# Long FFT convolution and phase mixing on Trainium2: the start of the kernel, with its trigonometric tables, written anew

## Chip, cores and metric

The kernel runs on one core of one Trainium2 chip. The metric is device microseconds of one execution; the median of three runs stands for a kernel. A time is compared with the kernel before, run on the same chip.

## What is computed

Eight sequences of 5696 tokens with 128 channels are convolved causally, channel by channel, with a filter `h` of the same length. The result goes through a phase mixing layer.

```python
def _attn_ref(x, h):                      # x (8, 5696, 128), h (5696, 128)
    L = 2 * S
    y = np.fft.irfft(np.fft.rfft(x, n=L, axis=1) * np.fft.rfft(h, n=L, axis=0)[None], n=L, axis=1)[:, :S, :]
    return y

def _moe_ref(x, w_theta, w_tok_r, w_tok_i, w_ch):
    theta = x @ w_theta
    zr, zi = x * np.cos(theta), x * np.sin(theta)
    y = np.einsum('ts,bsd->btd', w_tok_r, zr) + np.einsum('ts,bsd->btd', w_tok_i, zi)
    u = x + y
    return u + np.maximum(u @ w_ch, 0.0)
```

The output is that of the second function on the result of the first, in float32.

## The kernel before

**The convolution** is a Fourier transform of length 11392 = 178 x 64 in matrix multiplications. The inputs are cut into eight groups (two sequences, half the channels), and `h` is handled first as if it were a group. A group goes through four stages. *Stage a* (`stage_a`, L198) multiplies 89 rows by a table `f1_t` of 90 frequencies: 16 chunks of four matmuls (L207), each evicted from PSUM with 128x720 elements (L212 on VectorE or L214 on ScalarE). *Stage f2* (`f2`, L217) does the 64-point transform and the twiddle factors in one: for each of the 90 frequencies a weight of its own from `w_t2`, four matmuls of 64 rows a frequency (L225), eight frequencies a chunk, so 12 chunks, the last with two frequencies. After the last chunk the function issues 12 matmuls of 384 columns whose results nobody uses (L231, `WARM`), into the same PSUM tile as the last chunk; that chunk's eviction comes after them. For `h` the chunks are evicted, alternating between ScalarE (L262) and VectorE (L260), and written to HBM (L267, two transfers a chunk on SP's queue); for a group of `x`, *stage b* (`stage_b`) evicts them on ScalarE (L323), multiplies them on VectorE (L325, L330) by the spectrum of `h`, which SP's queue reads back (L316, two transfers a chunk, four chunks ahead), and fills `uv_t`. *Stages c and d* (L346 and following) transform back with tables `r_u`, `r_v`, `e_t` and the signs `sgn`. PSUM has four buffers for all of this.

**The tables.** All of them are sines and cosines of a turn, built on the chip. `turns_of` (L156) makes an index with an iota on GpSimd (L163), scales it there to a fraction of a turn (L165), and takes the nearest whole turn off on VectorE (L168, L169). `sine` is a ScalarE activation (L173); `cosine` takes the absolute value on VectorE (L176) and then an activation (L180). `w_table(k0)` (L190) does this for 15 frequencies of `w_t2`, 15 x 64 = 960 columns, and writes the negative of the sine with L195; six of them cover the 90 frequencies. The tiles `turn` and `whole` have two buffers each. A weight of `w_t2` is 128 rows (two copies of 64) by three blocks of 64 columns: sine, cosine, minus sine.

**The order.** The program writes: `f1_t`, three `w_table`, the copy of `h` into `h16` (L245, one instruction), the loads of x for groups 0 and 1 (`load_x`, L143, 16 transfers each on GpSimd's queue, which cast to 16 bits), stage a of `h` with the other three `w_table` woven in, the 12 chunks of f2 for `h` (`h_chunk`), then stage a of group 0 with `r_table`, `s_table` and the first loads of the spectrum woven in, and stage b of group 0 with three `e_table` woven in. The compiler's planner is free to put independent instructions of an engine in another order; the trace shows the order that it chose. From `setup.close()` (L403) on, the loop over the groups weaves stages c and a, then b and d. The program's later part has a stretch in which VectorE keeps its written order (`manual_schedule`, L949); the setup has none.

**The mixing** takes what is left: weights are streamed through a ring (L530), transposed on VectorE (L731), and multiplied in seven products in place of eight (L1116). It is not touched.

Of the kernel before, what the change touches and what calls it, by code (L numbers as in the profile page):

```python
# [10 lines left out]
F32 = mybir.dt.float32  # L11
BF16 = mybir.dt.bfloat16
F16 = mybir.dt.float16
add = mybir.AluOpType.add
# [8 lines left out]
def kernel(  # L23
# [10 lines left out]
    nc = tc.nc  # L34
# [48 lines left out]
    EN = N2 // 2 + 1  # L83
    WARM = 12
    XP = HD + 2
    assert N1 * N2 == NF and NB * N2 == S and NB % 2 == 1 and K1 <= P
    CHK = [(c0, min(CK, K1 - c0)) for c0 in range(0, K1, CK)]
    NCK = len(CHK)
# [14 lines left out]
    def pool(name, bufs, stack, **kw):  # L103
        return stack.enter_context(tc.tile_pool(name=name, bufs=bufs, **kw))
# [6 lines left out]
    fc = pool("fft_c", 1, conv, side="right")  # L111
    fs = pool("fft_s", 2, conv, side="right")
    s1 = pool("set_1", 1, setup, side="right")
    s2 = pool("set_2", 2, setup, side="right")

    uv_t = fc.tile([P, 2 * UVW + P], F16)
    u_t, v_t = uv_t[:, :UVW + P], uv_t[:, UVW:]
# [9 lines left out]
    def load_x(g, after=None):  # L127

        bp, dh = divmod(g, 2)
        if g >= B:  # L130
            return []
        if g not in x16s:
            x16s[g] = fx.tile([P, 2, N2, XP], F16, tag="x16", name="x16")
        x16 = x16s[g]

        def piece(i):
            e, n0 = i // 4, i % 4 * 16
            src = x[2 * bp + e]
            if after is not None:
                g_ = after["g"]  # L140
                nc.gpsimd.tensor_copy(x16[0:1, e, n0, 0:1], g_[0:1, 0, 16 * i:16 * i + 1])  # L141
            for p0, p1 in ((0, 80), (80, NB)):
                nc.gpsimd.dma_start(  # L143
                    x16[p0:p1, e, n0:n0 + 16, :HD],
                    bass.AP(tensor=src.tensor, offset=src.offset + (p0 * N2 + n0) * D + dh * HD,
                            ap=[[N2 * D, p1 - p0], [D, 16], [1, HD]]))
        return [lambda i=i: piece(i) for i in range(8)]

    lane = fc.tile([P, 2], F32)
    for p0 in (0, 64):  # L150
        nc.gpsimd.iota(lane[p0:p0 + 64, 0:1], pattern=[[0, 1]], base=0, channel_multiplier=1,
                       allow_small_or_imprecise_dtypes=True)
    nc.gpsimd.iota(lane[:, 1:2], pattern=[[0, 1]], base=0, channel_multiplier=1,
                   allow_small_or_imprecise_dtypes=True)

    def turns_of(pattern, base, lanes, m, per, quarter=None):  # L156

        n = 1
        for _, c in pattern:
            n *= c  # L160
        t = s2.tile([P, 11 * NB], F32, tag="turn", name="turn")[:m, :n]
        k = s2.tile([P, 11 * NB], F32, tag="whole", name="whole")[:m, :n]
        nc.gpsimd.iota(k, pattern=pattern, base=base, channel_multiplier=0,  # L163
                       allow_small_or_imprecise_dtypes=True)
        nc.gpsimd.tensor_scalar(t, k, lanes, 1.0 / per, op0=mult, op1=mult)  # L165
        if quarter is not None:
            quarter(t)
        nc.vector.tensor_scalar(k, t, MAGIC, None, op0=add)  # L168
        nc.vector.scalar_tensor_tensor(t, k, MAGIC, t, op0=ALU.subtract, op1=ALU.subtract)  # L169
        return t, k  # L170

    def sine(out_, r, sign):
        nc.scalar.activation(out_, r, AF.Sin, bias=zero_b[:r.shape[0]], scale=-sign * TWO_PI)  # L173

    def absolute(k, r):
        nc.vector.scalar_tensor_tensor(k, r, -1.0, r, op0=mult, op1=ALU.max)  # L176

    def cosine(out_, r, k):
        absolute(k, r)
        nc.scalar.activation(out_, k, AF.Sin, bias=half_pi[:r.shape[0]], scale=-TWO_PI)  # L180

    f1_t = fc.tile([P, 2 * K1], F16)
    t, k = turns_of([[1, K1]], 0, lane[:NB, 1:2], NB, N1)
    sine(f1_t[:NB, K1:], t, -1)
    cosine(f1_t[:NB, :K1], t, k)

    w_t2 = keep.tile([P, K1, 3 * N2], F16, tag="keep", name="w_t2")
    assert WB + BT + 3 * P * 2 <= K1 * 3 * N2

    def w_table(k0):  # L190
        t, k = turns_of([[1, 15], [N1, N2]], k0, lane[:, 0:1], P, NF)
        t3, k3 = (z.rearrange("p (k n) -> p k n", n=N2) for z in (t, k))
        sine(w_t2[:, k0:k0 + 15, :N2], t3, 1)
        cosine(w_t2[:, k0:k0 + 15, N2:2 * N2], t3, k3)
        nc.vector.tensor_scalar(w_t2[:, k0:k0 + 15, 2 * N2:], w_t2[:, k0:k0 + 15, :N2],  # L195
                                -1.0, None, op0=mult)

    def stage_a(lhs, both=False):  # L198

        st = {}  # L200

        def chunk(q):
            if q == 0:
                st["a"] = fa.tile([P, 2 * K1, HD], F16, tag="a", name="a_")
            ps = psum()
            for i in range(4):
                nc.tensor.matmul(ps[:, i // 2, (i % 2) * 2 * K1:(i % 2 + 1) * 2 * K1], lhs(q + i), f1_t[:NB],  # L207
                                 start=True, stop=True)
            a_out = st["a"][:, :, q:q + 4].rearrange("p k (a q) -> p k a q", a=2)
            a_in = ps[:, :, :4 * K1].rearrange("p a (q k) -> p k a q", q=2)  # L210
            if both and q % 8:
                nc.vector.tensor_copy(a_out, a_in)  # L212
            else:
                nc.scalar.activation(a_out, a_in, AF.Copy)  # L214
        return [lambda q=q: chunk(q) for q in range(0, HD, 4)], st
# [19 lines left out]
    def woven(*lists):  # L235

        lists = [l if isinstance(l, tuple) else (l, 0.0, 1.0) for l in lists]
        steps = [(w0 + (i + 0.5) / len(l) * (w1 - w0), n, f)
                 for n, (l, w0, w1) in enumerate(lists) for i, f in enumerate(l)]
        for _, _, f in sorted(steps, key=lambda s: s[:2]):  # L240
            f()

    for k0 in (0, 15, 30):
        w_table(k0)
    nc.vector.tensor_copy(h16[:NB], u_t[:NB, :N2 * D].rearrange("p (n h d) -> p h n d", h=2, d=HD))  # L245
    for f in load_x(0) + load_x(1):
        f()
    steps, a_h = stage_a(lambda q: h16[:NB].rearrange("p h n d -> p (h n) d")[:, :, q], True)
    woven(steps, [lambda k0=k0: w_table(k0) for k0 in range(45, K1, 15)])

    hst = [t[:, :6 * D * CK].rearrange("p (c h d k) -> p c h d k", c=6, h=2, k=CK) for t in (u_t, v_t)]
    nc.gpsimd.memset(hst[(NCK - 1) // 6][:, (NCK - 1) % 6], 0.0)
# [1 line left out]
    def h_chunk(c):  # L254
        c0, ck = CHK[c]
        ps = f2(a_h, c)
        h_ = hst[c // 6][:, c % 6]
        dst = h_[:, :, :, :ck]
        if c % 2:
            nc.vector.tensor_scalar(dst, ps, 16.0 / NF, None, op0=mult)  # L260
        else:
            nc.scalar.activation(dst, ps, AF.Copy, scale=16.0 / NF)  # L262
        for cc, j in ((0, 0), (NCK - 1, CHK[-1][1] - 1)):
            if c == cc:
                nc.vector.tensor_scalar(dst[:, :, :, j], dst[:, :, :, j], 0.5, None, op0=mult)
        for ri in range(2):
            nc.sync.dma_start(  # L267
                hf_hbm[:, c, :, ri, :].rearrange("h p n -> p h n"),
                h_[64 * ri:64 * ri + 64].rearrange("p h d k -> p h (d k)"))

    for c in range(NCK):
        h_chunk(c)
    nc.gpsimd.memset(uv_t[:, 2 * UVW:], 0.0)

    r_u = fc.tile([P, P], F16)
    r_v = fc.tile([P, P], F16)
    e_t = fc.tile([P, EN, 2, NB], F16)
    sgn = fc.tile([P, N2], F32)

    def r_table(n_, r_):  # L280
        def quarter(t):
            for q0 in range(2):
                for q1 in range(2):
                    a_ = t[64 * q0:64 * q0 + 64, 64 * q1:64 * q1 + 64]
                    nc.vector.tensor_scalar(a_, a_, 0.25 * (1 + n_ + q0 - q1), None, op0=add)

        t, k = turns_of([[0, 2], [1, N2]], 0, lane[:, 0:1], P, N2, quarter)
        sine(k, t, 1)
        nc.vector.tensor_scalar(r_[:, :N2 + EN], k[:, :N2 + EN], 0.125, None, op0=mult)
        nc.vector.tensor_scalar(r_[:, N2 + EN:], k[:, N2 + EN:], -0.125, None, op0=mult)  # L290

    def e_table(n0):
        t, k = turns_of([[1, 11], [N2, NB]], n0, lane[:K1, 1:2], K1, NF)
        t3, k3 = (z.rearrange("p (n m) -> p n m", m=NB) for z in (t, k))
        sine(e_t[:K1, n0:n0 + 11, 1, :], t3, -1)
        cosine(e_t[:K1, n0:n0 + 11, 0, :], t3, k3)

    def s_table():
        t, k = turns_of([[0, 1]], 1, lane[:, 1:2], P, 2)
        absolute(k, t)  # L300
        nc.vector.tensor_scalar(k, k, -4.0, 1.0, op0=mult, op1=add)
        nc.vector.memset(sgn, 1.0)
        nc.vector.tensor_scalar(sgn[:, EN:], sgn[:, EN:], k, None, op0=mult)

    LEAD = 4

# [82 lines left out]
    zz_n, ZB = [0], 3  # L389
    groups = [(bp, dh) for bp in range(B // 2) for dh in range(2)]  # L390

    def front(g):
        if g >= len(groups):
            return [], [], []
        bp, dh = groups[g]
        x16 = x16s[g].rearrange("p b n d -> p (b n) d")
        steps, a_st = stage_a(lambda q: x16[:NB, :, q])
        return (steps, *stage_b(a_st, dh))

    a0, load0, b0 = front(0)  # L400
    woven(a0, [lambda: r_table(0, r_u), lambda: r_table(1, r_v), s_table] + load0)
    woven(b0, [lambda n0=n0: e_table(n0) for n0 in range(0, EN, 11)])
    setup.close()  # L403
    fg = pool("fft_g", 1, conv, side="right")

# [773 lines left out]
```

## Time and profile before

| | us |
|---|---|
| runs: lowest, median, highest | 2082.85, 2087.07, 2088.17 |
| the profiled execution, device time | 2088.55 |
| its span, first to last instruction | 2086.7 |
| granted TensorE clock over the span | 0.984 |
| TensorE (PE) busy | 1955.1 |
| VectorE (DVE), ScalarE (ACT), GpSimd (POOL) busy | 1587.1, 646.6, 972.5 |

PE is busy for 94% of the span. A profile names the matmul's records PE and the weight loads PEld. A line of the timeline has the start, the duration, the engine, the source line and the operation with its tiles and sizes, how many there were, and in brackets the idle time of the engine before it with what ended it. A run of like instructions is merged into one line. Lines of the view by stretches have, for each engine in turn, busy time and number of instructions, then the granted clock, the share of the DMA engines and the rate.

### The profile page before, as it was taken

How to read it: one execution, taken by the hardware profiler on the slowest of the kernel's cores; microseconds unless marked ns; L12 is line 12 of the kernel's file. 1: busy time of each engine (PE TensorE's matmuls, PEld its weight loads, DVE VectorE, ACT ScalarE, POOL GpSimd, SP SyncE). 2: the span in 40 equal slices, each digit the busy share in tenths (PEclk: the TensorE clock that was granted, in tenths of full speed). 3: DMA queues.
4: the chain of work that ended last, by engine and by line, in shares of the span. 5: the costliest groups of instructions: out<-in, count | busy, mean ns of one | idle time of the engine just before them, and what ended most of it. 6: DMA issues, size and time to landing. Idle time of an engine off the chain costs nothing.

```text
span 2086.7 us, 41598 instructions
## 1 busy us (share of the span) xinstructions
PE 1955.1 (94%) x15688; PEld 1083.5 (52%) x15865; DVE 1587.1 (76%) x2809; ACT 646.6 (31%) x979; POOL 972.5 (47%) x1773
## 2 busy tenths in 40 slices
PE   2698898888999999999999999899999999999998
PEld 2588888754444444444444444344444444444444
DVE  5777777776788887888876766876867777777767
ACT  3777787783332323233310000011111111111111
POOL 7334231247444545454566554445453545444450
PEclk9799999899999999999999999999999999999999
DMA  9499997989898989898999899869697978878693
GB/s 124 106 131 152 167 159 179 236 252 245 147 167 172 180 171 167 170 181 171 179 170 161 131 197 259 134 117 154 124 156 127 154 132 148 143 136 151 127 157 87
DMA packets 504489, 335.00 MB, mean 161 GB/s; under 512 B 184999, under 2 KB 457511, under 8 KB 503303
## 3 DMA queue, kind: packets, MB, share of 16 engines
q0 software_dynamic: 322208, 156.75, 59.3%
q1 hardware_dynamic: 176096, 164.05, 27.6%
q10 hardware_dynamic: 5984, 11.54, 1.6%
q8 instruction: 124, 2.03, 0.4%
q14 instruction: 77, 0.63, 0.1%
HBM read 377.11 MB, written 92.49 MB: 225 GB/s over the span
## 4 chain that ended last, share of the span: by engine, by line
PE 62%; DVE 4%; DMA 2%; issue 2%; POOL 1%; ACT 0%; DVEq 0%; POOLq 0%
PE m L1116 58%; DVE c L1123 2%; POOL ring L530 1%; DMA ring<-in_moe_w_tok_r_dram 1%; DVE b L672 1%; PE utp L811 1%; PE v L818 1%; PE m L1120 1%; DVE wt L731 1%; PE theta_ps L417 0%; PE tpz L759 0%; DMA wl<-in_moe_w_tok_i_dram 0%; PE m L1003 0%; DMA yT<-yt_hbm 0%; PE m L1037 0%
## 5 line engine op out<-in xcount | busy, mean ns | idle before, releaser
L530 POOL DMA_DIRECT2D ring<-in_moe_w_tok_i_dram x720 | 387.9, 546 | 659.9 <-DVE wt L731 579.2
L530 POOL DMA_DIRECT2D ring<-in_moe_w_tok_r_dram x720 | 386.5, 547 | 149.0 <-DVE wt L731 85.1
L731 DVE STREAM_TRANSPOSE wt<-ring 128x384 f32<-128x384 f32 (+2 forms) x720 | 358.6, 522 | 109.2 <-PE m L1116 71.2
L1116 PE MATMUL m<-b,wt 128*128 128x512 bf16 x1599 | 386.1, 380 | 4.1 <-DVE wt L731 1.7
L1116 PEld LDWEIGHTS <-wt 128*128 128x128 bf16 x1804 | 176.1, 98 | 219.4 <-DVE wt L731 7.5
L1123 DVE TENSOR_TENSOR c<-c,m 128x512 f32<-128x512 f32 x412 | 264.9, 668 | 0.4 <-PE m L1116 0.4
L813 ACT ACTIVATE ring<-utp 128x512 bf16<-128x512 bf16 x85 | 50.7, 597 | 582.2 <-PE utp L811 582.2
L346 PE MATMUL ps<-r_u,uv_t 128*128 128x128 f16 x1024 | 127.7, 221 | 7.7 <-DVE uv_t L330 4.9
L347 PE MATMUL ps<-r_v,uv_t 128*128 128x128 f16 x1024 | 126.6, 221 | 1.6 <-issue 1.2
L325 DVE TENSOR_TENSOR uv_t<-xs,hs 128x2048 f16<-128x2048 f16 x88 | 105.8, 1225 | 25.1 <-ACT xs L323 14.7
L1037 PE MATMUL m<-b,wt 128*128 128x512 bf16 x466 | 111.8, 386 | 8.9 <-DMA b<-z_hbm 4.3
L808 ACT ACTIVATE ub<-c 128x512 bf16<-128x512 f32 x88 | 55.1, 628 | 192.6 <-DMA ring<-in_moe_w_tok_r_dram 114.0
L143 POOL DMA_DIRECT2D x<-in_x_dram x128 | 96.9, 762 | 25.4 <-POOL x L141 12.6
L346 PEld LDWEIGHTS <-uv_t 128*128 128x128 f16 x1024 | 101.0, 99 | 7.1 <-DVE uv_t L330 6.6
L347 PEld LDWEIGHTS <-uv_t 128*128 128x128 f16 x1024 | 100.9, 99 | 5.0 <-issue 3.2
L323 ACT ACTIVATE xs<-ps 128x1024 f16<-128x1024 f32 x96 | 91.5, 984 | 33.1 <-DVE uv_t L325 19.0
L1037 PEld LDWEIGHTS <-wt 128*128 128x128 bf16 x528 | 51.3, 99 | 69.1 <-issue 7.7
L225 PEld LDWEIGHTS <-w_t 64*128 64x128 f16 x3240 | 61.3, 102 | 49.2 <-issue 23.5
L419 ACT ACTIVATE red<-theta_ps,magic 128x512 f32<-128x512 f32 (+1 forms) x46 | 31.6, 687 | 136.9 <-PE theta_ps L417 107.2
L761 ACT ACTIVATE ring<-tpz 128x512 bf16<-128x512 bf16 (+1 forms) x46 | 27.5, 597 | 131.5 <-PE tpz L759 114.9
L441 ACT ACTIVATE mag<-mag,half_pi 128x512 f32<-128x512 f32 (+1 forms) x90 | 65.0, 722 | 0.0
L672 DVE TENSOR_TENSOR b<-b 128x1024 bf16<-128x1024 bf16 x100 | 61.4, 680 | 0.0
(2898 smaller groups left out, 3772.8 us busy)
## 6 DMA issues: line engine op xcount, KB each, us to landing
ring<-in_moe_w_tok_r_dram POOLq DMA_DIRECT2D x352, 96.0 KB, 4.5
ring<-in_moe_w_tok_i_dram POOLq DMA_DIRECT2D x352, 96.0 KB, 5.0
ring<-in_moe_w_tok_r_dram POOLq DMA_DIRECT2D x352, 80.0 KB, 4.3
ring<-in_moe_w_tok_i_dram POOLq DMA_DIRECT2D x352, 80.0 KB, 3.8
hs<-hf_hbm SPq DMA_DIRECT2D x192, 128.0 KB, 3.3
cp_hbm<-c SPq DMA_DIRECT2D x88, 256.0 KB, 2.5
c<-cp_hbm SPq DMA_DIRECT2D x88, 256.0 KB, 4.3
out_dram<-c SPq DMA_DIRECT2D x88, 256.0 KB, 4.0
```

The costliest lines, as they stand in the source:

```text
L143: nc.gpsimd.dma_start(x16[p0:p1, e, n0:n0 + 16, :HD], bass.AP(tensor=src.tensor, offset=src.offset + (p0 * N2 + n0) * D + dh * HD, ap=[[N2 ...
L323: nc.scalar.activation(xs[:, :, :, :ck], ps, AF.Copy)
L325: nc.vector.tensor_tensor(uv[:, :, :, c0:c0 + ck], xs.rearrange("p e d k -> p e (d k)").unsqueeze(1).to_broadcast([P, 2, 2, HD * CK]), hv. ...
L346: nc.tensor.matmul(o, u_t[:, at:at + P], r_u, start=True, stop=False)
L347: nc.tensor.matmul(o, v_t[:, at:at + P], r_v, start=False, stop=True)
L441: nc.scalar.activation(mag, mag, AF.Sin, bias=half_pi[:m], scale=-TWO_PI)
L530: nc.gpsimd.dma_start(wb[32 * i:32 * i + 32, :ng, :nj * 64], bass.AP(tensor=a.tensor, offset=a.offset + row0 * S + p * H + i * QR + j0 * 6 ...
L672: return [lambda f=f, x=x: f(*x) for f, x in ((nc.vector.tensor_sub, (bt[M3], b12, b22)), (nc.vector.tensor_sub, (bt[M4], b21, b11)), (nc. ...
L731: nc.vector.transpose(wt.rearrange("p j t r -> p (j t r)").bitcast(F32).rearrange("p (j g t) -> p g j t", j=TJ, g=4)[:, :ng, :nj], wb[:, : ...
L1037: nc.tensor.matmul(ms[n // 2 * 2 + h], a[n][:, j, :, r], bts_of[p][jj][n % 2 * 2 + h][:, r, :], start=(n % 2 == 0 and jj == 0 and r == 0), ...
L1116: nc.tensor.matmul(ms[q], a[q][:, j, :, r], bts[jj][q][:, r, :], start=(jj == 0 and r == 0), stop=(jj == NJ - 1 and r == 1 and q not in left))
L1123: nc.vector.tensor_tensor(c, z, ms[q], op=op)
```

## The change

Only the setup is edited, from the first instruction to the end of stage b of group 0.

- GpSimd, ScalarE and VectorE keep their written order in this part (`manual_schedule`, closed after stage b of group 0).
- The index of a table is made once; the angles of a table are then one instruction on GpSimd (`turns_of`), which is separate from the reduction on VectorE (`within`). Buffers: three for `turn`, two for `whole`.
- `w_t2` is built in three parts of 30 frequencies by 32 columns (960 elements, `w_angles`); `w_rest` writes the negative, and the other 32 columns of all three blocks as a product with a sign per partition.
- The absolute value is a bitwise AND with one source in place of the maximum of two.
- GpSimd's angles for `f1_t` and the whole of `w_t2` come before any load of x; the loads of group 0 next; then the angles of `r` and `e`; then the loads of group 1.
- The copy of `h` is cut into four by channels, between chunks of stage a.
- Evictions: in stage a of `h` and of group 0, chunks with n mod 5 = 1 or 3 on VectorE, the other 10 on ScalarE (before: 8 and 8 for `h`, all on ScalarE for group 0); in f2 of `h` every third on VectorE in place of every second.
- `r_table`, `s_table` and the first `e_table` are written before stage a of group 0; the second is woven into stage a, the third into stage b.

```diff
-    s2 = pool("set_2", 2, setup, side="right")
+    s2 = pool("set_2", 3, setup, side="right")
+    s3 = pool("set_3", 2, setup, side="right")
...
+    ordered = ExitStack()
+    ordered.enter_context(tc.manual_schedule(engines={
+        mybir.EngineType.DVE, mybir.EngineType.Activation, mybir.EngineType.Pool}))
+    lane = fc.tile([P, 6], F32)
...
+    for n, (col, per) in enumerate(((1, N1), (0, NF), (0, N2), (1, NF))):
+        nc.gpsimd.tensor_scalar(lane[:, n + 2:n + 3], lane[:, col:col + 1], 1.0 / per, None, op0=mult)
...
+    def index(pattern, tag):
...
+        k = s1.tile([P, n], F32, tag=tag, name=tag)
+        nc.gpsimd.iota(k, pattern=pattern, base=0, channel_multiplier=0, allow_small_or_imprecise_dtypes=True)
+        return k
+    def turns_of(k, base, of, m, tag=None):
...
+        nc.gpsimd.tensor_scalar(t, k[:m], float(base), of[:m], op0=add, op1=mult)
+        return t
+    def within(t):
+        k = s3.tile([P, 11 * NB], F32, tag="whole", name="whole")[:t.shape[0], :t.shape[1]]
         nc.vector.tensor_scalar(k, t, MAGIC, None, op0=add)
         nc.vector.scalar_tensor_tensor(t, k, MAGIC, t, op0=ALU.subtract, op1=ALU.subtract)
-        return t, k
+        return k
...
     def absolute(k, r):
-        nc.vector.scalar_tensor_tensor(k, r, -1.0, r, op0=mult, op1=ALU.max)
+        nc.vector.tensor_scalar(k.bitcast(mybir.dt.uint32), r.bitcast(mybir.dt.uint32), 0x7FFFFFFF, None,
+                                op0=ALU.bitwise_and)
...
+    k_w = index([[1, WK], [N1, H2]], "k_w")
+    t_w = [turns_of(k_w, WK * c, of_n2, P) for c in range(3)]
...
-    def w_table(k0):
-        t, k = turns_of([[1, 15], [N1, N2]], k0, lane[:, 0:1], P, NF)
...
+    def w_angles(c):
+        k = within(t_w[c])
+        absolute(k, t_w[c])
+        w_ = w_t2[:, WK * c:WK * c + WK, :]
+        sine(w_[:, :, :H2], t_w[c].rearrange("p (k n) -> p k n", n=H2), 1)
+        cosine(w_[:, :, N2:N2 + H2], k.rearrange("p (k n) -> p k n", n=H2))
+    def w_rest(c):
+        w_ = w_t2[:, WK * c:WK * c + WK, :]
+        nc.vector.tensor_scalar(w_[:, :, 2 * N2:2 * N2 + H2], w_[:, :, :H2], -1.0, None, op0=mult)
+        w_ = w_.rearrange("p k (c u n) -> p k c u n", c=3, u=2)
+        nc.vector.tensor_scalar(w_[:, :, :, 1], w_[:, :, :, 0], sign, None, op0=mult)
...
-            if both and q % 8:
+            if both and q // 4 % 5 % 2:
...
-    for k0 in (0, 15, 30):
-        w_table(k0)
-    nc.vector.tensor_copy(h16[:NB], u_t[:NB, :N2 * D].rearrange("p (n h d) -> p h n d", h=2, d=HD))
-    for f in load_x(0) + load_x(1):
+    for f in load_x(0):
         f()
+    nc.gpsimd.memset(uv_t[:, 2 * UVW:], 0.0)
+    k_r = index([[0, 2], [1, N2]], "k_r")
+    t_r = [turns_of(k_r, 0, of_r, P, f"t_r{n}") for n in range(2)]
+    k_f = within(t_f1)
...
+    signs()
+    w_angles(0)
+    w_angles(1)
+    w_rest(0)
+    def h_copy(d0):
...
+    h_copy(0)
+    w_rest(1)
     steps, a_h = stage_a(lambda q: h16[:NB].rearrange("p h n d -> p (h n) d")[:, :, q], True)
-    woven(steps, [lambda k0=k0: w_table(k0) for k0 in range(45, K1, 15)])
+    for n, f in enumerate(steps):
+        if n in (1, 3, 5):
+            h_copy(8 * n + 8)
+        if n == 6:
+            w_angles(2)
+        if n == 12:
+            w_rest(2)
+        f()
...
-        if c % 2:
+        if c % 3 == 1:
             nc.vector.tensor_scalar(dst, ps, 16.0 / NF, None, op0=mult)
...
-    a0, load0, b0 = front(0)
-    woven(a0, [lambda: r_table(0, r_u), lambda: r_table(1, r_v), s_table] + load0)
-    woven(b0, [lambda n0=n0: e_table(n0) for n0 in range(0, EN, 11)])
+    k_e = index([[1, 11], [N2, NB]], "k_e")
+    t_e = [turns_of(k_e, 11 * n, of_e, K1) for n in range(3)]
+    for f in load_x(1):
+        f()
+    r_table(0, r_u)
+    r_table(1, r_v)
+    s_table()
+    e_table(0)
+    a0, load0, b0 = front(0, True)
+    for f in load0:
+        f()
+    woven(a0, [lambda: e_table(1)])
+    woven(b0, [lambda: e_table(2)])
+    ordered.close()
```

## The prediction

> **What bounds the kernel now.** The chain of waits that ended last and the row of PE come first, then the view by stretches, then the timeline of the first 100 us.
>
> ```profile
> PE   2698898888999999999999999899999999999998
> ...
> PE 62%; DVE 4%; DMA 2%; issue 2%; POOL 1%; ACT 0%; DVEq 0%; POOLq 0%
> ```
>
> TensorE carries the chain and is full in nearly every slice of 52 us; only the first two, the setup, are not. By stretches, the setup and all behind it:
>
> ```profile
> 0.00:99.50 99.50, 46.99 (x881) 39.24 (x882) 63.12 (x91) 56.09 (x67) 56.96 (x79) 0.91 0.92 113
> 99.50:2086.70 1987.20, 1908.13 (x14808) 1044.27 (x14985) 1523.99 (x2719) 590.54 (x913) 915.57 (x1694) 0.99 0.89 163
> ```
>
> PE is idle for 52.5 us of the first 99.5 and for 79 us of the other 1987. Group 0's stage c begins at 99.47; everything behind it is timed relative to that point (no wait refers to a fixed time), so the change is worth what it moves that point. PE in the timeline:
>
> ```profile
> 26.44 0.76 PE L207 MATMUL ps<-f_t,h 89*128 89x180 f16 x4 [0.89 <-ACT a__182 L214]
> 31.53 4.42 PE L225 MATMUL ps<-a__182,w_t 64*128 64x64 f16 x159 [4.33 <-DVE a__182 L212]
> ...
> 53.49 1.78 PE L225 MATMUL ps<-a__182,w_t 64*128 64x64 f16 x60 [16.10 <-ACT w_t L180]
> 56.51 1.78 PE L225 MATMUL ps<-a__182,w_t 64*128 64x64 f16 x60 [1.24 <-DVE w_t L195]
> 61.99 1.78 PE L225 MATMUL ps<-a__182,w_t 64*128 64x64 f16 x60 [3.69 <-ACT w_t L180]
> 63.70 4.02 PE L231 MATMUL ps<-w_t 128*128 128x384 f16 x12
> ```
>
> Stage f2 of `h` stops after 45 frequencies and waits 16.10 + 1.24 + 3.69 = 21.0 us for the other three parts of `w_t2`. Why they are late is on GpSimd:
>
> ```profile
> 22.23 1.06 POOL L165 TENSOR_SCALAR turn<-whole,lane 128x960 f32<-128x960 f32 x1
> 23.36 17.28 POOL L143 DMA_DIRECT2D x<-in_x_dram  x23
> 41.01 1.50 POOL L143 DMA_DIRECT2D x<-in_x_dram  x2 [0.37 <-DMA x<-in_x_dram]
> 43.34 1.50 POOL L143 DMA_DIRECT2D x<-in_x_dram  x2 [0.83 <-DMA x<-in_x_dram]
> 44.84 1.97 POOL L163 IOTA whole<- 128x960 f32 x2
> 46.91 2.68 POOL L165 TENSOR_SCALAR turn<-whole,lane 128x960 f32<-128x960 f32 x2
> 48.00 0.66 DVE L168 TENSOR_SCALAR whole<-turn 128x960 f32<-128x960 f32 x1 [11.61 <-POOL turn L165]
> 48.69 1.90 DVE L169 SCALAR_TENSOR_TENSOR turn<-whole,turn 128x960 f32<-128x960 f32 x1
> ```
>
> The fourth part's index stands behind 27 issues of loads of x, at 17.28/23 = 0.75 us each.
>
> **The change, up to the end of the dummy matmuls (67.72 before).** GpSimd in the written order: small work until 3.46, four scalings (0.27 at most by L165's 128x1 row; 0.2 taken), index and angle of `f1_t` 0.24 + 0.35, index of w 1.02, three angles of 1.07: 9.3. Then 16 issues x 0.75 = 12.0, to 21.3.
>
> VectorE: a part of w costs L168 0.65 + L169 1.15 + the AND. The trace has no AND; it lies between 0.65 (L168, one source, same size) and 1.15 (L176, which it replaces). I take 0.65, the row with its number of sources: 2.45 a part. `w_rest` is L195's 0.41 and a product of 2880 elements, between 0.81 (L245's 8192 in 2.29) and 1.24 (three times L195); 0.95 taken, 1.36 together. A quarter of L245 is 0.57 at its rate, 2.45 at that of L176 (960 in 1.15) if rows of 16 elements lose it; 0.65 taken, since it is the same copy. With the first angle at 6.9, two parts end at 11.8, the first `w_rest` at 13.1, the first quarter of `h` (landed by 12.69 before) at 13.8. L169 took 1.90 beside GpSimd's L165 at 46.91, so I add 0.7: PE starts at 14.5 (15.04 before).
>
> Stage a of `h`: VectorE has 1.36 + 3 x 0.65 + 6 x 0.89 (L212) + 2.45 + 1.36 = 12.5; ScalarE 10 x 0.77 (L214) + 2 x 1.10 = 9.9. Laid out chunk by chunk with four PSUM buffers, one engine sometimes waits for the other: 13.9, to 28.4 (31.5 before). All of `w_t2` is then there. Stage f2 is 11.25 chunks x 0.89 (159 matmuls in 4.42, 32 a chunk) = 10.0; the evictions (7 x 1.02 + 0.4 on ScalarE, 4 x 1.24 on VectorE) hide under it. Dummies 4.02. End: **42.4, a gain of 25.3**.
>
> Work costed at nothing: the loads of group 0, which must have landed at 42.4. The last is issued at 21.3 and the median load lands 5.4 us after its issue, 26.7: 15.7 us of cover, beyond which each microsecond counts in full. [...]
>
> **From the dummies to the end of stage a of group 0 (11.3 us before).** Here written order costs. VectorE's halving of the last chunk of `h` (L265) needs that chunk's eviction, which waits for the dummies; in written order `r_table`, `s_table` and the first `e_table` queue behind it, and ScalarE's evictions of stage a, with PE behind four full buffers, behind those. Eviction and halving 0.95; two `r_table`, each 4 x 0.15 (L285) + 0.23 + 0.29 + ScalarE 0.40 + 0.38 = 1.9; signs 0.35; `e_table` 0.66 + 1.16, then sine and cosine 1.2 each: 9.3 until ScalarE's first eviction (0.5 before, since those tables were made while PE waited for w). Then ten evictions of 0.67 (16 in 10.72 before) and two activations of the second `e_table`, 9.1, with the hand-overs to VectorE 11.3. Together 20.6, **a loss of 9.3**, ending at 63.0.
>
> **Stage b of group 0 (20.5 before).** First chunk and its eviction 2.0, then VectorE's 11 x 1.24 (L325) + 0.71 (L330) + 2.5 for the last `e_table`, and 0.3 for a wait such as the 0.9 for `hs` before: 19.3, **a gain of 1.2**. ScalarE has one `e_table` less beside it than it had. On SP's queue the 24 writes of the spectrum (L267: 13.94/14 = 1.0 us each at most) start near 30.5 and end near 53.5; eight reads (6.28/8) end at 59.8 and land by 62.5, ahead of the first product at 65.0. This cover is thin, 2.5 us. Group 1's loads follow the angles of e (1.1 + 3 x 1.47) on GpSimd, from about 29 to 41, and are wanted near 78.
>
> **Sum:** -25.3 + 9.3 - 1.2 = -17.2. The profiled execution of 2088.55 (span 2086.7) becomes 2071.35; the median lies 1.48 below it, at 2087.07, and becomes **2070**.
>
> Bounds: the AND at 1.15 adds 0.5 at five places on the path, 2.5; quarter copies at 2.45 add 5.4 (three inside stage a); products 0.9; waits between VectorE and GpSimd such as that 1.90 could add 3: together 12, 2082. Downward, TensorE might already be faster: matmuls of stage a cost 5.65/36 = 0.157 us before the dummies and 2.04/20 = 0.102 behind them; f2 and the dummies at 0.7 of their time would give 4: 2066.
>
> **The rivals.** *The tables of r and e are hidden*, because VectorE and ScalarE reach them while PE still does f2. For it: both have spare time in that stretch (5 of 10 us for VectorE, by the evictions above). Against it: L265 of the last chunk is written ahead of them. The 9.3 would shrink to 1: 2062.
>
> *VectorE becomes the bound of the setup*: it already has 12.5 us of work in a stage a of 13.9, so that upper prices go straight onto the path. For it: L168 to L195 were busy 16.44 of 16.5 us from 15.0 to 31.5. 2077 to 2084.
>
> *The rest is planned anew and comes out worse*, the one way to slower that I find; in the setup alone even the upper bounds end stage b at 94.5, before 99.47. After `ordered.close()` the planner starts from other engine states, and VectorE and ScalarE in groups 1 to 7 are 80% busy (16.86 and 15.79 of 20 us from 120 to 140), so that a poorer order would show. It decides from 17.2/7 = 2.5 us a group; at 4 us the time is 2087 - 17 + 28 = 2098. Against it: the written text of those stages is the same, and PE's text order is kept by its waits.
>
> *The change does not do what it says*: the angles of w could still wait for buffers. They have three `turn` tiles of their own for three parts, so I see no such wait; the time would be near 2087.
>
> **Chances.** Forecast (2064 to 2077) 0.62; hidden tables 0.12; VectorE-bound 0.17, of which 0.05 above 2081; poorer plan 0.06; no effect 0.03. A difference of less than 0.3%, 6.3 us, can't be told from none (the three runs span 5.3). Faster 0.62 + 0.12 + 0.12 = 0.86, same 0.05 + 0.03 = 0.08, slower 0.06. The range 2059 to 2083 holds the forecast, most of the VectorE case and the hidden tables' own 2062.
>
> **What the profile after would show.** No wait of PE L225 for `w_t2` above 1 us; the dummies of `h` near 38.4 to 42.4; a hole of PE of 7 to 9 us behind them, ended by ScalarE's first eviction of group 0; the first L346 near 82; the stretch from there to the end 1987 us long. Wrong if that last stretch differs by more than 5 us, if the AND or the quarter copies take over 1 us, or if stage a of group 0 waits for a load of x.

## The result, and the profile after

The changed kernel takes 2075.64 us (median of six runs, 2068.87 to 2083.55) against 2088.24 (2082.85 to 2092.04) for the kernel before in the same comparison. The ratio is 0.9944, 95% interval 0.992 to 0.9969: 12.6 us by the medians, 6.5 to 16.7 by the interval. The forecast of 2070 was 5.6 us too low; 1.2 of that is the time before, 2088.24 here for the 2087.07 it was worked out from. The profiled execution of after took 2068.87 (span 2067.1), the fastest of its six, so its 19.6 us of difference in span is more than the change is worth. A second profile of the same kernel, among the experiments, shows by how much.

TensorE by slices of 52 us and the shares of the chain that ended last, after:

```profile
PE   4788998889999999999999999999999999999998
...
PE 63%; DVE 5%; issue 2%; POOL 2%; DMA 1%; ACT 0%; DVEq 0%; POOLq 0%
```

TensorE still carries the chain; its first two slices, 2 and 6 before, are 4 and 7. The view by stretches, cut where stage c of group 0 begins (busy time by engine, granted clock, DMA share, GB/s):

```profile
0.00:84.76 84.76, 43.21 (x880) 37.70 (x881) 60.15 (x88) 49.00 (x59) 47.09 (x70) 0.84 0.96 133
84.76:2067.10 1982.34, 1904.81 (x14808) 1042.83 (x14985) 1524.77 (x2719) 590.20 (x912) 917.61 (x1694) 0.99 0.89 163
```

Stage c begins at 84.76 in place of 99.47: 14.71 us come from the setup. The rest is 4.86 us shorter, although nothing in it was edited. The traces' records of the granted clock put it at half for 48.5 us of the rest before and for 35.8 after; matmuls of stage a took 0.163 us each at 0.50 and 0.088 at 1.00 (after, 52.52 and 43.70), so that by estimate a TensorE busy throughout loses 0.46 of the difference, 5.8 us, enough for the 4.86. The first such stretch of before, 98.70 to 105.53, covers the start of stage c of group 0. One row around it, and then one of after:

```profile
99.00:105.83 6.83, 6.36 (x58) 6.30 (x59) 3.18 (x5) 2.78 (x4) 1.10 (x2) 0.52 0.50 122
```

```profile
84.76:103.87 19.11, 19.11 (x314) 18.87 (x316) 13.58 (x12) 14.21 (x22) 9.49 (x18) 1.00 0.96 94
```

That stage took 21.9 us before and 19.1 after. So of the 19.6 us, 14.7 are the setup and about 5 are the rest, for which the clock is enough by that estimate.

TensorE in the timeline of after (start, duration, line, idle time before it and what ended it):

```profile
17.72 2.65 PE L238 MATMUL ps<-f_t,h 89*128 89x180 f16 x16 [17.72 <-DVE h L289]
...
32.49 6.80 PE L256 MATMUL ps<-a__184,w_t 64*128 64x64 f16 x287 [1.48 <-DVE a__184 L243]
40.58 1.24 PE L256 MATMUL ps<-a__184,w_t 64*128 64x64 f16 x73 [1.28 <-issue]
41.74 2.12 PE L262 MATMUL ps<-w_t 128*128 128x384 f16 x12
43.70 1.41 PE L238 MATMUL ps<-f_t,x 89*128 89x180 f16 x16
...
52.52 5.22 PE L238 MATMUL ps<-f_t,x 89*128 89x180 f16 x32 [7.41 <-DVE a__784 L243]
...
77.51 1.30 PE L256 MATMUL ps<-a__784,w_t 64*128 64x64 f16 x40 [5.92 <-ACT xs L372]
```

The waits of f2 of `h` for `w_t2`, 21.0 us before, are gone. Two holes are new: 7.41 us behind the dummies and 5.92 us in stage b. On GpSimd the angles of all of `w_t2` now end at 10.0, ahead of the 16 loads of group 0:

```profile
6.50 3.50 POOL L178 TENSOR_SCALAR turn<-k_w,lane 128x960 f32<-128x960 f32 x3
9.95 13.83 POOL L145 DMA_DIRECT2D x<-in_x_dram  x16
```

ScalarE shows what both holes have in common:

```profile
50.98 1.11 ACT L189 ACTIVATE e_t<-turn,zero_b 90x979 f16<-90x979 f32 x1 [2.49 <-DVE turn L185]
52.01 1.11 ACT L196 ACTIVATE e_t<-whole,half_pi 90x979 f16<-90x979 f32 x1
53.02 3.37 ACT L245 ACTIVATE a__784<-ps 128x720 f16<-128x720 f32 x5
...
74.43 1.11 ACT L189 ACTIVATE e_t<-turn,zero_b 90x979 f16<-90x979 f32 x1 [3.54 <-DVE turn L185]
75.45 1.11 ACT L196 ACTIVATE e_t<-whole,half_pi 90x979 f16<-90x979 f32 x1
76.47 1.90 ACT L372 ACTIVATE xs<-ps 128x1024 f16<-128x1024 f32 x2
```

It stands still before the sines of these two tables until VectorE has reduced their angles, 2.49 and 3.54 us, and the evictions that TensorE needs are written behind the sines.

### The profile page after: what moved, and what is told of

The parts are those of the page before. It is cut to its first block, busy times and chain, and to the rows that moved or that the text cites. A ratio compares the mean times of both kernels' runs of the same rounds, so it can differ in the third digit from the quotient of the medians.

```text
span 2067.1 us, 41585 instructions
## 1 busy us (share of the span) xinstructions
PE 1948.0 (94%) x15688; PEld 1080.5 (52%) x15865; DVE 1584.9 (77%) x2806; ACT 639.2 (31%) x971; POOL 964.7 (47%) x1764
## 4 chain that ended last, share of the span: by engine, by line
PE 63%; DVE 5%; issue 2%; POOL 2%; DMA 1%; ACT 0%; DVEq 0%; POOLq 0%
PE m L1176 58%; PE m L1097 2%; DVE c L1183 2%; POOL ring L590 1%; DVE b L732 1%; PE v L878 1%; PE utp L871 1%; PE m L1180 1%; DMA ring<-in_moe_w_tok_i_dram 1%; DVE wt L791 1%; PE theta_ps L477 0%; PE tpz L819 0%; PE m L1063 0%; DMA ring<-in_moe_w_tok_r_dram 0%; POOL wl L838 0%
## 5 line engine op out<-in xcount | busy, mean ns | idle before, releaser
L238 PE MATMUL ps<-f_t,x 89*128 89x180 f16 x512 | 59.7, 255 | 8.8 <-DVE a__784 L243 8.7
```

## Experiments

The theory: the gain comes from the angles ahead of the loads, it is carried unchanged to the end, and the written order of the r and e tables gives a part of it back. The rivals: the tables' instructions or the evictions, not the loads, made the gain; or the rest was planned anew. Ratios are to the kernel before on the same chip; "stage c" is the start of group 0's stage c in the one profile (99.47 before, 84.76 after).

**The changed kernel again**, unedited.

> The changed kernel once more, unedited, for a closer ratio. Theory A (the setup's gain is carried to the end): group 0's stage c starts near 84.8 us as in the first profile, and the time is 12 to 18 us below the kernel before; what varies between executions behind that point is the number of stretches in which TensorE is granted half its clock. Rival B (the first profile was a lucky one and the change gains little): the ratio comes out above 0.997.

Measured: 2073.84, ratio 0.9943 [0.993, 0.9956], stage c at 88.21, the rest 1985.09 us with 41.8 us at half clock. Both miss what theory A expected (84.8, and 12 to 18 us), and rival B's ratio above 0.997 did not come either. The 11.3 us gained ahead of stage c agree with the 10.9 of the medians; the first profile's 14.7 was a lucky one. Of the 3.45 us between the two profiles 2.39 are there by the end of the dummies: the gap marked "issue" in f2 of `h` 2.00 us for 1.28, the 73 matmuls behind it 2.00 for 1.24, the dummies 2.92 for 2.12. Another 1.2 us come in stage b, where the hole of 5.92 is 7.41 us in this run.

**Before, with only the loads of x moved** behind the calls of `w_table`.

```diff
-    for f in load_x(0) + load_x(1):
-        f()
     steps, a_h = stage_a(lambda q: h16[:NB].rearrange("p h n d -> p (h n) d")[:, :, q], True)
     woven(steps, [lambda k0=k0: w_table(k0) for k0 in range(45, K1, 15)])
+    for f in load_x(0):
+        f()
...
     for c in range(NCK):
         h_chunk(c)
     nc.gpsimd.memset(uv_t[:, 2 * UVW:], 0.0)
+    for f in load_x(1):
+        f()
```

> The kernel before with only its loads of x written later: group 0's behind the six table calls, group 1's behind the last chunk of the spectrum of h. Theory A (the 21 us wait for w_t2 came from GpSimd's 27 issues of loads ahead of the last three parts): the wait of 16.1 us shrinks below 3 us, the dummies of h end near 47 instead of 67.7, group 0's stage c starts at 78 to 84 us, and the time falls by 14 to 20 us, as much as the whole change gives. Rival C (the gain is the halved table work and the cheaper instructions): stage c of group 0 starts above 94 us and the time falls by less than 5 us.

Measured: 2082.97, ratio 0.9988 [0.9977, 0.9999]. TensorE's longest wait for `w_t2` fell from 16.10 to 3.75 us, the dummies ended at 52.96 (67.72 before), and stage c began at 84.83, as early as in the changed kernel. Yet only some 2.5 us (0.12% of 2085, with an interval that reaches to 0.01%) arrived at the end: stage c of group 0 took 32.9 us in place of 21.9. Theory A held for the start of stage c, within 1 us, and failed for the time; rival C held for the time alone. GpSimd and then VectorE in this run:

```profile
58.39 0.45 POOL L163 IOTA whole<- 128x128 f32 x2
...
78.90 0.14 POOL L163 IOTA whole<- 128x1 f32 x1 [14.48 <-DVE r_u L292]
...
91.52 1.11 POOL L163 IOTA whole<- 90x979 f32 x1 [2.02 <-ACT e_t L180]
```

```profile
96.32 1.18 DVE L176 SCALAR_TENSOR_TENSOR whole<-turn 90x979 f32<-90x979 f32 x1
98.69 3.48 DVE L356 TENSOR_TENSOR g__1373<-ps,sgn 90x1024 f16<-90x1024 f32 x3 [1.19 <-ACT e_t L180]
```

The index of the last e table now came at 91.52, and the first eviction of stage c, which waits for that table, at 98.69. The wait had moved to the next tables. The loads in front of them are not the whole of it: the angles of r were ready at 59.8, but VectorE, idle for 12.23 us before 66.27, took them up only at 75.58, behind most of stage b's products, where the planner had put them. GpSimd, with two buffers for a table, stood 14.48 us for that before it could make the index of the next one. Nearly all of the early start was lost again, so moving the loads alone is not the change's gain. That the other tables have to come early too, as the change has it, follows from this run but was not tried by itself.

**Full tables**: six parts of 15 by 64, no mirroring, the rest as after.

```diff
-    WK = 30
+    WK = 15
...
-    H2 = N2 // 2
+    H2 = N2
...
-    t_w = [turns_of(k_w, WK * c, of_n2, P) for c in range(3)]
+    t_w = [turns_of(k_w, WK * c, of_n2, P) for c in range(6)]
...
-        w_ = w_.rearrange("p k (c u n) -> p k c u n", c=3, u=2)
-        nc.vector.tensor_scalar(w_[:, :, :, 1], w_[:, :, :, 0], sign, None, op0=mult)
...
-        if n == 6:
-            w_angles(2)
-        if n == 12:
-            w_rest(2)
+        if n in (6, 8, 10):
+            w_angles(n // 2)
+        if n in (8, 10, 12):
+            w_rest(n // 2 - 1)
```

> The changed kernel with w_t2 made as before in six parts of 15 frequencies by 64 columns, without the mirroring by sign; its angles still stand ahead of the loads of x, and written order is kept. Theory A (the halved tables spare VectorE 4.6 us, 6 x 2.5 + 6 x 0.4 against the 12.7 measured, and GpSimd three angles, in a stage a that VectorE bounds): the dummies of h begin 3 to 7 us later than at 41.7, and stage c of group 0 starts at 87 to 92 in place of 84.8 to 88.2. Rival F (the table work hides under the arrival of h and the evictions): that start moves by less than 2 us.

Measured: 2078.55, ratio 0.9968 [0.9955, 0.9981], stage c at 91.73. TensorE starts at 19.94 (17.72) and f2 of `h` at 38.11 (32.49). Against the unedited repeat the ratio is 0.0025 worse: halving is worth some 5 us (the two intervals just touch). All of it is there when f2 of `h` starts, 2.2 us ahead of stage a of `h` and 3.4 in it, and VectorE's rows follow one another without a gap from 5.4 to 36.3.

**Old eviction shares**: 8 and 8 in stage a of `h`, every second chunk of f2, all of group 0's stage a on ScalarE.

```diff
-            if both and q // 4 % 5 % 2:
+            if both and q % 8:
...
-        if c % 3 == 1:
+        if c % 2:
...
-    a0, load0, b0 = front(0, True)
+    a0, load0, b0 = front(0)
```

> The changed kernel with the shares of evictions of before: 8 and 8 in stage a of h, 6 and 6 in its f2, all sixteen on ScalarE in stage a of group 0. Theory A: stage a of group 0 is then 16 x 0.67 + 2.2 = 12.9 us of ScalarE in place of ten, so it ends about 2.5 us later, and stage c of group 0 starts 1 to 4 us later than in the changed kernel. Rival G (the shares decide nothing, since the spectrum's reads on SP's queue set the pace of stage b): less than 1 us.

Measured: 2081.02, ratio 0.9982 [0.9971, 0.9993], stage c at 94.18. The shares are worth some 8 us (0.0039 of 2085), more than expected. Part is ahead of f2 of `h`, which starts at 34.98 (32.49) since VectorE ends stage a of `h` later. The unexplained pause in f2 of `h` is 3.88 us here, for 1.28 and 2.00 in the two profiles of the changed kernel, and so a part of the late stage c that the shares need not have caused. The larger part is stage a of group 0, TensorE in this run:

```profile
51.04 1.41 PE L238 MATMUL ps<-f_t,x 89*128 89x180 f16 x16
60.93 5.36 PE L238 MATMUL ps<-f_t,x 89*128 89x180 f16 x32 [8.49 <-ACT a__784 L245]
68.19 2.73 PE L238 MATMUL ps<-f_t,x 89*128 89x180 f16 x16 [1.90 <-ACT a__784 L245]
```

With every eviction on the engine that must first make the sines, the hole grows to 8.49 us, and stage a, from its first matmul to f2 of group 0, takes 21.8 us in place of 19.2.

**The r, s and first e tables written between the chunks of h**, with their angles.

```diff
-    r_table(0, r_u)
-    r_table(1, r_v)
-    s_table()
-    e_table(0)
...
+    then = {2: lambda: r_table(0, r_u), 4: lambda: r_table(1, r_v), 5: s_table, 7: lambda: e_table(0)}
     for c in range(NCK):
         h_chunk(c)
+        if c in then:
+            then[c]()
```

> The changed kernel with r_table, s_table and the first e_table written between the chunks of stage f2 of h in place of behind them. Theory A (the hole of 7.4 us of TensorE behind the dummies is these tables, queued in written order behind the halving of the last chunk): the hole falls below 1.5 us, f2 of h gets up to 2 us longer, and stage c of group 0 starts 5 to 8 us earlier, near 78. Rival D (the hole is the loads of x of group 0, or the evictions, and the tables only fill it): the start of that stage c stays within 2 us of 84.8.

Measured: 2071.2, ratio 0.9932 [0.9918, 0.9947], stage c at 84.20. The hole of 7.41 is gone and f2 of group 0 starts at 59.36 rather than 62.90, but stage b took most of it back. For the hole theory A held; the start of stage c moved by 0.6 us, which is what rival D expected. VectorE's first products:

```profile
62.71 2.36 DVE L381 TENSOR_TENSOR uv_t<-xs,hs 128x2048 f16<-128x2048 f16 x2 [4.74 <-DMA hs<-hf_hbm]
66.14 1.23 DVE L381 TENSOR_TENSOR uv_t<-xs,hs 128x2048 f16<-128x2048 f16 x1 [1.07 <-DMA hs<-hf_hbm]
```

They wait for the spectrum of `h`, which is still behind its 24 writes on SP's queue (35.41 to 55.40 in after): the thin cover of the prediction, used up as soon as the work before it was faster. ScalarE's first eviction ended near 61.5, so of the 4.74 us about 1.2 are the spectrum's alone.

**The same, with one write of 128 partitions a chunk.**

```diff
-        for ri in range(2):
-            nc.sync.dma_start(
-                hf_hbm[:, c, :, ri, :].rearrange("h p n -> p h n"),
-                h_[64 * ri:64 * ri + 64].rearrange("p h d k -> p h (d k)"))
+        nc.sync.dma_start(
+            hf_hbm[:, c].rearrange("h r p n -> (r p) h n"),
+            h_.rearrange("p h d k -> p h (d k)"))
...
```

> The kernel with the tables of r and e between the chunks of f2, and the two writes of a chunk of the spectrum of h merged into one of 128 partitions (12 issues on SP's queue in place of 24; the layout of the spectrum in HBM has real and imaginary parts outside the 64 rows). Theory A (what took back the gain of the tables was SP's queue: 24 writes of 0.83 us, and the reads of the spectrum behind them, with VectorE waiting 4.7 us for the first): the writes end some 8 us earlier, the first wait of VectorE for hs falls below 1 us, and stage c of group 0 starts at 77 to 81 in place of 84.2. Rival H (the DMA engines are full, at shares of 1.6 to 1.9, and not the issuing queue): the merged writes take as long in all, and that start moves by less than 1.5 us.

Measured: 2070.56, ratio 0.9935 [0.9915, 0.9954], stage c at 82.30. The first product starts at 62.55, only 0.16 us sooner, though the profile now puts its wait down to ScalarE; later waits for the spectrum are 0.31 and 0.80 (1.07, 0.56, 0.48 and 0.93). Stage c starts 1.9 us sooner, short of theory A's 77 to 81 and more than rival H's 1.5 us. TensorE still stands 5.86 us in stage b around the last e table, and the time is that of the run before.

**After, without the written order** (`manual_schedule` left out; the same instructions, ordered by the planner).

```diff
-    ordered.enter_context(tc.manual_schedule(engines={
-        mybir.EngineType.DVE, mybir.EngineType.Activation, mybir.EngineType.Pool}))
```

> The changed kernel without the rule that VectorE, ScalarE and GpSimd keep their written order in the setup. Theory A (in this setup written order costs at the seam between h and group 0 and buys little, since GpSimd's list is written ahead anyway): the planner moves some of the r and e tables ahead of the last chunk of h, the hole behind the dummies shrinks, and stage c of group 0 starts between 78 and 84. Rival E (written order is what brings the gain): the start of that stage c goes back above 90 us.

Measured: 2064.35, ratio 0.9905 [0.989, 0.9919], stage c at 78.53: the best so far. The planner put both r tables between the chunks of `h` (39.8 to 44.8 on VectorE) and all e tables ahead of stage b's first eviction. ScalarE at the e tables:

```profile
47.50 1.11 ACT L187 ACTIVATE e_t<-turn,zero_b 90x979 f16<-90x979 f32 x1 [0.72 <-DVE turn L183]
48.52 1.11 ACT L194 ACTIVATE e_t<-whole,half_pi 90x979 f16<-90x979 f32 x1
49.52 2.85 ACT L243 ACTIVATE a__782<-ps 128x720 f16<-128x720 f32 x4
52.27 1.11 ACT L187 ACTIVATE e_t<-turn,zero_b 90x979 f16<-90x979 f32 x1
```

It waits 0.72 us once and never before the other sines. With merged writes too:

> The planner's own order in the setup, as in the kernel without the rule of written order, with the same merged writes. Theory A (there SP's queue is the bound of stage b: five waits for hs, 7 us together): the start of stage c of group 0 falls from 78.5 to 73 to 76, and the time lies 2 to 5 us below the 2064.35 of that kernel. Rival H: within 1.5 us of it.

Measured: 2066.36, ratio 0.9907 [0.9893, 0.9921], stage c at 77.46; no measurable gain, as rival H expected, so the writes do not set the time here.

**What in the planner's order is better?** First its list was copied by hand: the last e table out of stage b into stage a, alone.

```diff
-    woven(a0, [lambda: e_table(1)])
-    woven(b0, [lambda: e_table(2)])
+    woven(a0, [lambda: e_table(1), lambda: e_table(2)])
+    woven(b0)
```

> The new kernel with one line of its written order changed: the last table of e is written among the evictions of stage a of group 0 instead of among the chunks of stage b. In the new kernel that table stops VectorE's products for 3.87 us of work and 2.40 us of waiting (last product before it ends at 72.6, the next starts at 77.49), and TensorE is empty for 5.9 us behind it. Theory A (the place in stage b costs because VectorE's products set the pace there, and ScalarE's evictions in stage a leave room): stage a ends some 3.3 us later (VectorE 1.2 + 0.7 idle in it is free, ScalarE's 2.2 are not), stage b is some 4.9 us shorter, and group 0's stage c begins 1 to 2 us earlier than in runs of the new kernel (84.8 and 88.2), near 83 to 86. Theory B (a table costs the same wherever it stands ahead of stage c): it begins within 1 us of 84.8 to 88.2, and the ratio stays at 0.994.

Measured: 2073.66, ratio 0.9946 [0.9933, 0.996], stage c at 87.34, as theory B expected: stage b is 3.3 us shorter (18.6 for 21.9) and stage a of group 0, to the start of its f2, 3.6 longer (22.8 for 19.2), ScalarE standing 2.14 us before the moved sines. Then the same line with the r, s and first e tables between the chunks of `h` and merged writes:

> The new kernel in written order, but with the list that the planner chose for itself in the run without a written order: both tables of r, the signs and the first table of e between the chunks of h, the second and third table of e among the evictions of stage a of group 0, none in stage b; the spectrum of h is written with one transfer a chunk. Theory A (it is the list that costs, not that it is fixed): group 0's stage c begins at 78 to 80 (82.3 with the last table of e in stage b, 77.5 for the planner's order with the same transfers) and the ratio is 0.990 to 0.992. Theory B (a fixed order costs because it cannot follow what is ready, and the planner's gain is spread over many small choices): stage c begins at 81 to 83 and the ratio stays at 0.993 to 0.994.

Measured: 2072.83, ratio 0.9944 [0.993, 0.9957], stage c at 82.72; theory B again. The planner's list in fixed order is not the planner's time. ScalarE in this run:

```profile
52.80 1.11 ACT L189 ACTIVATE e_t<-turn,zero_b 90x979 f16<-90x979 f32 x1 [2.57 <-DVE turn L185]
...
60.35 1.11 ACT L189 ACTIVATE e_t<-turn,zero_b 90x979 f16<-90x979 f32 x1 [2.15 <-DVE turn L185]
61.37 1.11 ACT L196 ACTIVATE e_t<-whole,half_pi 90x979 f16<-90x979 f32 x1
62.38 2.05 ACT L245 ACTIVATE a__772<-ps 128x720 f16<-128x720 f32 x3
```

**Each table cut in two**, from the last run: VectorE's part (`e_table`, `r_table`) written two to four chunks ahead of ScalarE's (`e_sines`, `r_sine`). Every instruction stays.

```diff
...
-    then = {2: lambda: r_table(0, r_u), 4: lambda: r_table(1, r_v), 5: s_table, 7: lambda: e_table(0)}
+    then = {1: lambda: r_table(0, r_u), 3: lambda: (r_sine(0, r_u), r_table(1, r_v)),
+            4: lambda: r_scale(0, r_u), 5: lambda: r_sine(1, r_v), 6: lambda: e_table(0),
+            7: lambda: (r_scale(1, r_v), s_table()), 8: lambda: e_sines(0), 10: lambda: e_table(1)}
...
-    woven(a0, [lambda: e_table(1), lambda: e_table(2)])
+    for n, f in enumerate(a0):
+        f()
+        for at, fn, m in ((2, e_sines, 1), (3, e_table, 2), (7, e_sines, 2)):
+            if n == at:
+                fn(m)
```

> The written order of the last run (all tables ahead of stage b, one write a chunk), but each table cut in two: VectorE's part (index reduced, absolute value) is written two to four chunks ahead of ScalarE's sines, so that ScalarE does not stand still in front of its sines. In the last run it stood 2.57 and 2.15 us before the sines of the second and third table of e, with evictions of stage a queued behind them, and 1.37, 1.74 and 1.80 us before those of r and of the first e, with evictions of h behind; in the planner's order only 0.72 once. Theory A (those stops are what the written order costs): dummies of h end near 45 (47.7), stage a of group 0 takes some 13 us (16.8), stage c of group 0 begins at 77.5 to 79.5 (82.7), ratio 0.990 to 0.992. Theory B (ScalarE had the room, and the cost lies in the load of VectorE or in the transfers of h): stage c begins at 81 to 83, ratio 0.993 to 0.995.

Measured: 2066.13, ratio 0.9916 [0.9894, 0.9938], stage c at 78.47. ScalarE at the second and third e table, with no idle time before the sines:

```profile
48.31 1.43 ACT L245 ACTIVATE a__776<-ps 128x720 f16<-128x720 f32 x2
49.63 1.12 ACT L189 ACTIVATE e_t<-turn,zero_b 90x979 f16<-90x979 f32 x1
50.63 1.12 ACT L196 ACTIVATE e_t<-whole,half_pi 90x979 f16<-90x979 f32 x1
51.65 2.07 ACT L245 ACTIVATE a__776<-ps 128x720 f16<-128x720 f32 x3
53.60 1.13 ACT L189 ACTIVATE e_t<-turn,zero_b 90x979 f16<-90x979 f32 x1
```

Stage a of group 0, with the hand-over to f2, takes 11.6 us for 16.9. Of these 5.3 us, 4.7 are ScalarE's two stops. The cut also takes VectorE's part of the second e table out of this stage, to 46.29 in f2 of `h`, and no run parts the two effects. The dummies ended at 47.90, not at the 45 expected: the gap marked "issue" in f2 of `h` was 3.39 us in this run. Theory A holds for stage a, and the ratio lies within its bounds, though its interval overlaps that of the run before. On the same chip, the freely ordered kernel once more:

> The new kernel without its written order, a second time, beside the split tables on the same chip. Theory A and theory B both expect the first value again: ratio 0.989 to 0.992, stage c of group 0 at 78 to 80 (78.53 in the first profile). If it comes out near 0.994, the order planned freely is no better than the written one, and the first result was one of fewer stretches at half of the clock.

Measured: 2065.03, ratio 0.9912 [0.9886, 0.9937], stage c at 77.85. The two can't be told apart. So a fixed order as such has no cost that shows here; what cost was writing ScalarE's sines directly behind the VectorE work that they wait for. Both versions beat the kernel before. Their ratios lie 0.0027 to 0.0038 below the repeat of the change, some 6 to 8 us; for the free order's first run that is clear of noise, for the split tables alone the intervals overlap.

No run takes only the order of angles and loads out of the changed kernel, so its own part of the gain stays open: the loads moved alone bring 2.5 us, and of the 11 to 13 us of the whole, some 5 go without the halved tables and some 8 without the shares.

## Why the prediction held, and where not

- **Up to the end of the dummies** 42.4 was predicted, 43.87 measured (46.26 in the second profile): a gain of 23.85 for 25.3. Four terms were off and partly cancelled, which was luck. TensorE started at 17.72, not 14.5. The largest piece, 1.5 us, is a term that the sum had at nothing: VectorE's eight small instructions for `f1_t` and the signs, 5.38 to 9.14, so that the first part of w began at 9.14, though its angle was there at 7.7 (6.9 in the sum). The rest are that later angle and longer rows beside GpSimd, for which 0.7 had been added (the first two L184 of w took 1.37 and 1.05 for 0.65, the first product 1.31 for 0.95; more in the last section). Stage a of `h` to the start of f2 took 14.8 for 13.9, f2 9.25 for 10.0, pause included, and the dummies 2.12 for 4.02, at a recorded clock of 1.00 (last section), a speed which the prediction had only as its downward bound. The AND at 0.66 was priced well, the quarter copies at 0.71 to 1.08 for 0.65 less so; one of the four passed the 1 us that the prediction had set as a sign of being wrong. GpSimd's terms add up to 9.1, not 9.3. The loads of group 0 were in time, as costed.
- **Written order behind the dummies**: ScalarE's first eviction of group 0 came 9.15 us after them (9.3 predicted), the hole was 7.41 (7 to 9 predicted), though VectorE's first eviction, at 51.57, ended it, and stage a's last eviction ended 18.98 after them (20.6). This step held, and the experiments show its cause.
- **Stage b of group 0** was the step that failed: 21.9 us for 19.3 (its terms add up to 19.15), a loss of 1.4 for a gain of 1.2. The term "2.5 for the last `e_table`" counted VectorE's work and not that the sines stand before the next evictions on ScalarE. VectorE's last product before the table ended at 72.6 and the next began at 77.49, 4.9 us with 2.40 of waiting, in place of the 2.5 (and a hole of TensorE of 7.41 us in the second profile, for 5.92). The same effect had been counted in stage a and left out here.

```profile
77.49 4.74 DVE L374 TENSOR_TENSOR uv_t<-xs,hs 128x2048 f16<-128x2048 f16 x4 [2.40 <-ACT xs L372]
```

- **The cover on SP's queue** held: writes from 35.41, reads from 55.44, waits for the spectrum of 0.19 to 0.55. That it was thin was right too: it was gone when f2 of group 0 started 3.5 us sooner.
- **The rest, 1987.2** in the prediction: 1982.3 and 1985.1, the first 4.9 us off, just inside the 5 that the prediction allowed. The half-clock time, 48.5 us before, 35.8 and 41.8 after, is enough for that by the estimate above; a new plan of the rest need not be assumed. The planner rival fell.
- **Hidden tables** as a rival was put at 2062 with the objection that L265 of the last chunk is written ahead. The objection was right for this order. With the tables moved between the chunks of `h` the time was 2071, since stage b took the gain back; cut in two as well, or ordered by the planner, it was 2064 to 2066.
- **VectorE as the bound** came true in part, as the 3.2 us by which TensorE started late and the 0.9 us more in stage a of `h`. The 16.44 us of the prediction's row for it are all of VectorE's work there, evictions included. **No effect** fell.

Of the 17.2 us of the sum, 12.6 and 10.9 came by the two medians, and the start of stage c moved by 14.7 and 11.3 in the two profiles. In the first profile the 2.5 us short are 1.45 lost by the end of the dummies and 2.6 in stage b, less 1.6 won in stage a of group 0. In the second, another 3.45 were lost, as told above.

## What to carry to other kernels

When a wait on a table is taken away by putting it ahead in its queue, look at what the next tables wait for: in the run with the loads alone moved, 14.6 us were won at one table and nearly all lost at the next. Where one engine prepares and a second finishes, both in written order, write the preparation a few chunks ahead of the finish; here the second engine's idle time before that instruction (2.49 and 3.54 us in after) was paid by the evictions behind it. A setup's gain is best read as the move of one milestone, in more than one profile.

## What the hardware showed

In these traces the granted clock was at half in stretches of 3.41 us, from 41.58 in the repeat of after, and of two, six and five times that: 6.83 from 98.70 before, 20.48 from 48.14 in after, 17.07 from 51.82 in its repeat. In after, the stretch began 3 us into the hole of 7.41 us and outlasted it; the view from 52.50 to 62.85:

```profile
52.50:62.85 10.35, 7.88 (x48) 6.98 (x48) 6.64 (x8) 9.29 (x13) 0.79 (x2) 0.50 0.73 199
```

It stayed at half for 16 us after TensorE had resumed at 52.52, busy for 7.88 of the 10.35 us in the row. What set its length is not shown. Between the two profiles of the changed kernel, the end of f2 of `h` and the dummies alone differ by 1.56 us, with the clock at 0.50 from 41.58 to 44.99 in the repeat and at 1.00 there in after.

The 1.00 that the view reads at the start of these traces does not go with the speed of a recorded 1.00. The records begin at 67.98 us before and at 37.90 in after, and ahead of them a matmul of stage a took 0.165 us (3.96 for 24, at 20.57 in after), about as at 0.50 (0.163: 5.22 for 32, at 52.52), and 0.088 at a recorded 1.00 (1.41 for 16, at 43.70). So the 12 dummies of `h` took 4.02 us before, ahead of the first record, and 2.12 in after, behind it.

Some of VectorE's smallest instructions took several times as long as others of their size while GpSimd made the index and the angles of w, 5.32 to 10.0 (VectorE in after):

```profile
6.78 0.96 DVE L192 TENSOR_SCALAR whole<-t_f 89x90 uint32<-89x90 uint32 x1
...
7.82 0.15 DVE L211 TENSOR_SCALAR s_k<-s_t 128x1 f32<-128x1 f32 x1
8.01 0.83 DVE L212 SCALAR_TENSOR_TENSOR s_t<-s_k,s_t 128x1 f32<-128x1 f32 x1
...
9.14 1.37 DVE L184 TENSOR_SCALAR whole<-turn 128x960 f32<-128x960 f32 x1
```

One element a partition took 0.15 or 0.83 us, and 90 elements 0.96, where the instruction just ahead of it took 0.25. The first step on `f1_t`, also 90 elements, took 1.08 at 5.38, beside GpSimd's index of w, for 0.20 before. GpSimd's three angles took 1.17 each from 6.50. What made some rows long and others not is not shown. GpSimd's loads, beside VectorE's work on w, differed little: the 16 of group 0 took 0.86 us each for 0.75 (1.8 us in sum), and ended 2.5 us later than predicted.

In f2 of `h`, TensorE paused before its 288th matmul in all twelve profiles of the changed kernel and the versions made from it, 1.28 to 3.88 us, with nothing in the trace that it waited for. Its cause stays open.
